# Moving the transposes of q, k and the masked scores from TensorE to the DMA crossbar in an attention and tanh-shrink kernel

## The chip, the cores and the metric

The kernel runs on one core of a Trainium2 chip. The metric is the device time of one execution in microseconds. A time is the median of the executions named with it. Nearly all executions here are fast. Where one or two of them were slow, the text says so and compares the fast ones.

## The reference

Eight batches of eight heads, 576 positions, 64 columns a head. Scores more than `tau` below their row's maximum are masked out, the rest go through a softmax. The output is the input of two layers with `h - tanh(h)` between them.

```python
scores = scale * np.matmul(q, k.transpose(0, 1, 3, 2))          # scale = 1/8
thresh = np.max(scores, axis=-1, keepdims=True) - tau           # tau = 0.02
scores = np.where(scores >= thresh, scores, -1000000000.0)
scores = scores - np.max(scores, axis=-1, keepdims=True)
attn = np.exp(scores); attn = attn / (np.sum(attn, axis=-1, keepdims=True) + 1e-09)
x = np.matmul(attn, v)                                          # then heads side by side: 4608 x 512
h = x @ w_in                                                    # 512 x 2048
out = (h - np.tanh(h)) @ w_out                                  # 2048 x 512
```

## The kernel before

Heads are taken in 32 pairs, each of nine score tiles: four of 128 rows for each head ("A" and "B" in turn, a duo), and a middle one, "M", with the last 64 rows of both. A row of scores has 576 columns. For exactness q and k are split into a high and a low fp16 half, side by side in 128 columns, and the scores add the products with `kT` and with `kS`, which is `kT` with its halves exchanged.

TensorE turns q and k by transposes into PSUM, VectorE copies them to SBUF, and two small DMAs make `kS`:

```python
def turn(p, t):
    hl = hls.pop((p, t))
    ps = ps_big.tile([P, W], FP16, name=f"ps_{t}", tag="big")          # W = 1152
    for c in range(TPP):                                               # TPP = 9
        nc.tensor.matmul(out=ps[:, c * P : (c + 1) * P], lhsT=..., rhs=ident_f16, is_transpose=True, ...)
    m = qk_pool.tile([P, W], FP16, name=f"{t}T", tag=t)
    nc.vector.tensor_copy(out=m, in_=ps)
    ...                                                                # first pair: cut
    elif t == "k":
        nc.sync.dma_start(out=sw[0:D, :], in_=m[D:P, :])
        nc.sync.dma_start(out=sw[D:P, :], in_=m[0:D, :])
```

A row maximum gives the threshold; `kink` writes the masked scores `z` (kept columns are score minus threshold, the others hugely negative). `weights` transposes `z` on TensorE into the single PSUM buffer `psZ`, and ScalarE takes the exponential from there:

```python
def weights(i):
    ps = ps_z.tile([P, 5 * P], BF16, name="psZ", tag="z")
    ...
    for c in range(n):                                                 # n = 4 or 5
        nc.tensor.matmul(out=ps[:, c * P : (c + 1) * P], lhsT=z[...], rhs=ident_bf, is_transpose=True, ...)
    nc.scalar.activation(out=pt[:, off : off + n * P], in_=ps[:, 0 : n * P], func=ACT.Exp)
```

One slot of the main loop handles one tile: scores three tiles ahead, `kink` one ahead, `weights`, a share of the layers of the batch before (from pair 4 on), and the product with v. All loads and stores go through the SP queue, but for the very first load of q.

Of the kernel before, what the change touches and what calls it, by code (L numbers as in the profile page):

```python
# [9 lines left out]
F32 = mybir.dt.float32  # L10
# [8 lines left out]
def kernel(  # L19
# [33 lines left out]
    AHEAD = 3  # L53
# [7 lines left out]
    ident_f16 = const.tile([P, P], FP16, name="ident_f16")  # L61
    make_identity(nc, ident_f16)
# [3 lines left out]
    xT = const.tile([P, DM_C, B, S], BF16, name="xT")  # L66
# [5 lines left out]
    NV = 3  # L72
# [8 lines left out]

    pool = lambda name, bufs, **kw: ctx.enter_context(
# [5 lines left out]
    qk_pool = pool("qk", 2)  # L88
    sc_pool = pool("sc", AHEAD + 1)
    st_pool = pool("st", 8)  # L90
    z_pool = pool("z", 3)
# [5 lines left out]
    y_pool = pool("y", 2)  # L97
    ps_big = pool("ps_big", 2, space=PSUM)
    ps_z = pool("ps_z", 1, space=PSUM)
    ps_o = pool("ps_o", 1, space=PSUM)  # L100
    ps_h = pool("ps_h", 1, space=PSUM)
# [9 lines left out]
    def load(p):  # L111
        b, h0 = p // HPAIR, 2 * (p % HPAIR)
        hs = slice(h0, h0 + 2)
        for t, src in (("k", k), ("q", q)):
            eng = nc.scalar if p == 0 and t == "q" else nc.sync
            r = raw_pool.tile([P, 10, D], F32, name=f"{t}raw", tag=t)
            eng.dma_start(
                out=r.rearrange("p (h c) d -> p h (c d)", h=2)[:, :, 0 : 4 * D],
                in_=src[b, hs, 0:512, :].rearrange("h (p c) d -> p h (c d)", c=4),
            )  # L120
            eng.dma_start(out=r[:, 4, :], in_=src[b, hs, 512:S, :])
            raws[p, t] = r
        r = raw_pool.tile([P, 10, D], F32, name="vraw", tag="v")
        nc.sync.dma_start(
            out=r[:, 0:8, :].rearrange("p (h c) d -> p h (c d)", h=2),
            in_=v[b, hs, 0:512, :].rearrange("h (p c) d -> p h (c d)", c=4),
        )
        rem = v[b, hs, 512:S, :].rearrange("h s d -> s h d")
        nc.sync.dma_start(out=r[0:64, 8:10, :], in_=rem)
        nc.sync.dma_start(out=r[64:P, 8:10, :], in_=rem)  # L130
        raws[p, "v"] = r
# [3 lines left out]
    def split(p, t, fast=False):  # L135
        r = raws.pop((p, t))[:, 0:9, :]
        hl = hl_pool.tile([P, TPP, 2, D], FP16, name=f"{t}hl", tag=t)
# [6 lines left out]
        else:  # L144
            x = hl_pool.tile([P, TPP, D], F32, name="xs", tag="xs")
# [7 lines left out]
        hls[p, t] = hl  # L153

    def split_v(p):
        r, vb = raws.pop((p, "v")), vbs[p % NV]
        nc.gpsimd.tensor_copy(
            out=vb[:, :, 0:4, 0:D],
            in_=r[:, 0:8, :].rearrange("p (h c) d -> p h c d", h=2),
        )  # L160
        nc.gpsimd.tensor_copy(out=vb[0:64, :, 4, 0:D], in_=r[0:64, 8:10, :])
        nc.gpsimd.tensor_copy(out=vb[64:P, :, 5, 0:D], in_=r[64:P, 8:10, :])
# [5 lines left out]
    def turn(p, t):  # L168
        hl = hls.pop((p, t))
        ps = ps_big.tile([P, W], FP16, name=f"ps_{t}", tag="big")  # L170
        for c in range(TPP):
            nc.tensor.matmul(  # L172
                out=ps[:, c * P : (c + 1) * P],
                lhsT=hl[:, c, :, :].rearrange("p a d -> p (a d)"),
                rhs=ident_f16, is_transpose=True, start=True, stop=True,
            )
        m = qk_pool.tile([P, W], FP16, name=f"{t}T", tag=t)
        nc.vector.tensor_copy(out=m, in_=ps)  # L178
        mats[p, t] = m
        if t == "k" and p == 0:  # L180
            ps = ps_big.tile([P, W], FP16, name="ps_ks", tag="big")
            for c in range(TPP):
                for a in range(2):
                    nc.tensor.matmul(
                        out=ps[64 * a : 64 * a + 64, c * P : (c + 1) * P],
                        lhsT=hl[:, c, 1 - a, :],
                        rhs=ident_f16, is_transpose=True, start=True, stop=True,
                    )
            sw = qk_pool.tile([P, W], FP16, name="kS", tag="ks")
            nc.vector.tensor_copy(out=sw, in_=ps)  # L190
            mats[p, "ks"] = sw
        elif t == "k":
            sw = qk_pool.tile([P, W], FP16, name="kS", tag="ks")
            nc.sync.dma_start(out=sw[0:D, :], in_=m[D:P, :])
            nc.sync.dma_start(out=sw[D:P, :], in_=m[0:D, :])
            mats[p, "ks"] = sw
# [4 lines left out]
    scs, zs, pts, ops = {}, {}, {}, {}  # L201
# [5 lines left out]
    def scores(i):  # L207
# [29 lines left out]
        )  # L237
        nb = st_pool.tile([P, 1], F32, name="nb", tag="nb")
# [5 lines left out]
    def kink(i):  # L244
        sc, nb = scs.pop(i)
        kd = kind(i % TPP)
        if kd == "B":
            z = zs[i - 1][:, S:W]
        else:
            zt = z_pool.tile([P, W], BF16, name="z")  # L250
            zs[i] = zt
            z = zt[:, 0:S]
        nc.scalar.activation(  # L253
            out=z, in_=sc, func=ACT.Prelu, bias=nb, scale=1.0, alpha=STEEP
        )

    def weights(i):

        kd = kind(i % TPP)
        ps = ps_z.tile([P, 5 * P], BF16, name="psZ", tag="z")  # L260
        if kd == "B":
            z, pt, off, n = zs.pop(i - 1), pts[i - 1], 512, 5
        else:
            z = zs[i] if kd == "A" else zs.pop(i)
            pt = p_pool.tile([P, TPP * P], FP16, name="pT")
            pts[i] = pt
            off, n = 0, 4
        for c in range(n):
            nc.tensor.matmul(  # L269
                out=ps[:, c * P : (c + 1) * P],  # L270
                lhsT=z[:, off + c * P : off + (c + 1) * P],
                rhs=ident_bf, is_transpose=True, start=True, stop=True,
            )
        if kd == "M":
            nc.tensor.matmul(
                out=ps[0:64, 512:640], lhsT=z[:, 512:576],
                rhs=ident_bf, is_transpose=True, start=True, stop=True,
            )
        nc.scalar.activation(  # L279
            out=pt[:, off : off + n * P], in_=ps[:, 0 : n * P], func=ACT.Exp  # L280
        )
        if kd == "M":
            nc.scalar.activation(
                out=pt[0:64, 512:640], in_=ps[0:64, 512:640], func=ACT.Exp
            )

    def attend(i):
# [19 lines left out]
        pt, hh = pts.pop(i - 1), int(j > 4)  # L307
# [24 lines left out]

    def emit_x(p):
        o = osb.pop(p)
        ps = ps_z.tile([P, S], BF16, name="psX", tag="z")
# [13 lines left out]
        nc.vector.tensor_copy(out=xT[:, p % HPAIR, b, :], in_=ps)  # L349


    gs = {}

    def hidden(m, n, ps):
        if n == 0:
            gs[m] = g_pool.tile([P, DF_C, MB], BF16, name="g")
        for c in range(DM_C):
            nc.tensor.matmul(  # L358
                out=ps, lhsT=w_in_sb[:, c, n * P : (n + 1) * P],
                rhs=xT[:, c, m, 0:MB] if m < B else xT[:, c, :, MB:S],  # L360
                start=(c == 0), stop=(c == DM_C - 1),
            )
        th = t_pool.tile([P, MB], F32, name="th")
        nc.scalar.activation(out=th, in_=ps, func=ACT.Tanh)  # L364
        nc.vector.scalar_tensor_tensor(  # L365
            out=gs[m][:, n, :], in0=th, scalar=-1.0, in1=ps,
            op0=ALU.mult, op1=ALU.add,
        )

    def project(m, ms, part, ps, last):  # L370
# [5 lines left out]
        if part == 3:  # L376
# [5 lines left out]
            if m < B:  # L382
                rows = out[m * S : m * S + MB, :].rearrange("(p c) n -> c p n", c=4)
                nc.sync.dma_start(out=rows[ms], in_=yo)
            else:
                rows = out.rearrange("(b s) n -> b s n", b=B)
                nc.sync.dma_start(out=rows[2 * ms : 2 * ms + 2, MB:S, :], in_=yo)

    def layers(m, tail):
# [3 lines left out]
        def h_step(n):  # L393
            if tail and n % 3:
                ps = ps_big.tile([P, MB], F32, name="psHt", tag="big")
            else:
                ps = ps_h.tile([P, MB], F32, name="psH", tag="h")
            hidden(m, n, ps)

        def y_step(ms, part):  # L400
            if part == 0:
                tag = ("y", "o", "z")[(4 * (m - 1) + ms) % 3] if tail else "y"
                pl = {"y": ps_y, "o": ps_o, "z": ps_z}[tag]
# [38 lines left out]

    load(0)
    load(1)
    for t in ("k", "q"):
        split(0, t, fast=True)
        turn(0, t)
# [6 lines left out]
    for s in range(-AHEAD, NTILE + 4):  # L454
        p, j = divmod(max(s, 0), TPP)
        if 0 <= s < NTILE and j == 3 and p % HPAIR == 0 and p >= HPAIR:
            assert not todo
            todo = layers(stage, False)
            share = len(todo) / (HPAIR * TPP - 3)
            done, stage = 0.0, stage + 1  # L460
        if s + AHEAD < NTILE:
            scores(s + AHEAD)
        if 0 <= s + 1 < NTILE:
            kink(s + 1)
# [9 lines left out]
        if s - 1 == NTILE + 1:  # L474
            emit_x(NPAIR - 1)
        if 0 <= s - 1 < NTILE:
            attend(s - 1)
            pp, jj = divmod(s - 1, TPP)
# [4 lines left out]
            if jj == 1 and pp > 0:  # L483
                emit_x(pp - 1)
        if 0 <= s < NTILE:
            if j == 0 and p + 2 < NPAIR:
                load(p + 2)
            if p + 1 < NPAIR:
                if j == 0:
                    split(p + 1, "k")  # L490
                if j == 1:
                    split(p + 1, "q")
                if j == 2:
                    split_v(p + 1)
                    turn(p + 1, "k")
                if j == 4:
                    turn(p + 1, "q")
            if s in w_when:
# [6 lines left out]
    while stage <= NMB:  # L505
        for step in layers(stage, True):
            step()
        stage += 1
# [37 lines left out]
```

## Time and profile before

| | before |
|---|---|
| time | 646.99 us, median of 4 (646.28 to 647.18) |
| span of the profile | 644.8 us |
| mean granted TensorE clock | 0.99 |
| first copy of a pair's output to the transposed x | 34.7 us |
| pace, pairs 8 to 31 | about 17.8 us a pair |
| end of attention, then layers only | 560 us, then 85 us |

The copies of a pair's output to the transposed x (`xT`, one for each pair) serve as milestones: the time between two of them is the pace. The lines of this profile stand in the prediction. A line of a group ends with busy us, mean ns of one instruction, and the idle time of the engine before them with what ended it.

### The profile page before, as it was taken

The numbers are of one execution on the slowest core, as the hardware profiler recorded it, in microseconds if no ns is written. First come the engines' busy times: TensorE is split into PE (matmuls) and PEld (weight loads), VectorE is DVE, ScalarE is ACT, GpSimd is POOL, SyncE is SP. The second block draws the span as 40 slices with busy tenths as digits, with TensorE's granted clock in tenths as the row PEclk, the third lists the DMA queues.
The fourth block names the chain that finished last, engine by engine and source line by source line (L and its number), as shares of the span: only waits on it lengthen the run. The fifth ranks groups of instructions, "written<-read, shape, count | busy, mean of one in ns | idle before, by whom it ended". The sixth has DMA issues, their size and how long they took to land.

```text
span 644.8 us, 15693 instructions
## 1 busy us (share of the span) xinstructions
PE 594.6 (92%) x6048; PEld 362.0 (56%) x6130; DVE 459.5 (71%) x1274; ACT 461.6 (72%) x761; POOL 215.2 (33%) x309
## 2 busy tenths in 40 slices
PE   2988998989999999999999999999999999999990
PEld 2666655556566566656655656656665666544440
DVE  2888888887877777877778777877877777544410
ACT  1888888887778777787778787777778778533410
POOL 6267557733303730343313630362133400000000
PEclk9999999999999999999999999999999999999996
DMA  5565656432223331353133231353134201000111
GB/s 152 155 177 163 175 168 174 119 81 73 64 65 91 104 93 37 93 148 92 40 87 84 77 90 38 93 149 95 36 93 121 66 17 37 18 33 34 49 36 47
DMA packets 57139, 57.35 MB, mean 89 GB/s; under 512 B 20840, under 2 KB 45416, under 8 KB 57064
## 3 DMA queue, kind: packets, MB, share of 16 engines
q1 hardware_dynamic: 56662, 56.05, 30.8%
q8 instruction: 48, 0.79, 0.5%
q10 hardware_dynamic: 402, 0.29, 0.1%
q14 instruction: 27, 0.22, 0.1%
HBM read 37.75 MB, written 9.44 MB: 73 GB/s over the span
## 4 chain that ended last, share of the span: by engine, by line
PE 79%; ACT 9%; DVE 4%; issue 3%; DMA 2%; SPq 1%; ACTq 0%
PE psY L372 18%; PE psH L358 16%; PE psS L228 16%; PE psZ L269 10%; PE psO L313 5%; ACT pT L279 5%; ACT z L253 3%; PE ps_k L172 3%; PE psHt L358 3%; PE ps_q L172 2%; PE psS L218 2%; DVE sc L234 2%; PE psX L337 2%; DMA out_dram<-yo 2%; PE psO L301 1%
## 5 line engine op out<-in xcount | busy, mean ns | idle before, releaser
L279 ACT ACTIVATE pT<-psZ 128x512 f16<-128x512 bf16 (+1 forms) x288 | 184.6, 641 | 83.8 <-PE psZ L269 80.9
L253 ACT ACTIVATE z<-sc,nb 128x576 bf16<-128x576 f32 x288 | 221.3, 768 | 8.9 <-DVE nb L239 8.9
L234 DVE TENSOR_SCALAR_CACHE_REDUCE sc<-psS 128x576 f32<-128x576 f32 x288 | 216.2, 751 | 8.8 <-PE psS L228 7.8
L365 DVE SCALAR_TENSOR_TENSOR g<-th,psH 128x512 bf16<-128x512 f32 x124 | 85.3, 688 | 88.9 <-ACT th L364 88.9
L372 PE MATMUL psY<-w_out_sb,g 128*128 128x512 bf16 x540 | 138.2, 379 | 1.3
L269 PE MATMUL psZ<-ident_bf,z 128*128 128x128 bf16 x1280 | 118.8, 219 | 9.9 <-ACT pT L279 9.1
L358 PE MATMUL psH<-xT,w_in_sb 128*128 128x512 bf16 x451 | 118.1, 379 | 3.4 <-issue 1.3
L269 PEld LDWEIGHTS <-z 128*128 128x128 bf16 x1280 | 79.2, 98 | 52.2 <-issue 16.7
L228 PE MATMUL psS<-kT,qT 128*128 128x512 f16 (+1 forms) x512 | 105.8, 288 | 2.8 <-DVE qT L178 0.9
L228 PEld LDWEIGHTS <-qT 128*128 128x128 f16 x1024 | 74.2, 98 | 58.8 <-issue 5.2
L228 PE MATMUL psS<-kS,qT 128*128 128x512 f16 (+1 forms) x512 | 105.6, 288 | 0.0
L364 ACT ACTIVATE th<-psH 128x512 f32<-128x512 f32 x124 | 74.0, 597 | 35.9 <-PE psH L358 34.3
L146 POOL TENSOR_SCALAR xs<-kraw 128x576 f32<-128x576 f32 x31 | 20.8, 670 | 225.0 <-DMA kraw<-in_k_dram 159.1
L372 PEld LDWEIGHTS <-g 128*128 128x128 bf16 x576 | 51.8, 98 | 46.1
L358 PEld LDWEIGHTS <-w_in_sb 128*128 128x128 bf16 x576 | 51.0, 98 | 43.0 <-issue 0.8
L313 PEld LDWEIGHTS <-pT 128*128 128x128 f16 x1280 | 55.8, 98 | 22.4
L313 PE MATMUL psO<-vb,pT 128*128 128x65 bf16 x1280 | 61.2, 193 | 0.9
L239 DVE TENSOR_SCALAR nb<-mx 128x1 f32<-128x1 f32 x288 | 44.3, 154 | 10.0
L150 POOL TENSOR_TENSOR khl<-xs,khl 128x576 f16<-128x576 f32 x31 | 39.7, 1279 | 2.6
L150 POOL TENSOR_TENSOR qhl<-xs,qhl 128x576 f16<-128x576 f32 x31 | 39.6, 1279 | 2.6
L328 DVE TENSOR_TENSOR osb<-psO,rc 128x320 bf16<-128x320 f32 x64 | 29.3, 458 | 2.2
L178 DVE COPY qT<-ps_q 128x1152 f16<-128x1152 f16 x32 | 24.1, 754 | 9.2 <-PE ps_q L172 9.2
(53 smaller groups left out, 462.3 us busy)
## 6 DMA issues: line engine op xcount, KB each, us to landing
out_dram<-yo SPq DMA_DIRECT2D x36, 256.0 KB
kS<-kT SPq DMA_DIRECT2D x62, 144.0 KB
kraw<-in_k_dram SPq DMA_DIRECT2D x32, 256.0 KB
vraw<-in_v_dram SPq DMA_DIRECT2D x32, 256.0 KB
qraw<-in_q_dram SPq DMA_DIRECT2D x31, 256.0 KB
wt<-in_moe_w_in_dram SPq DMA_DIRECT2D x8, 512.0 KB
wt<-in_moe_w_out_dram SPq DMA_DIRECT2D x8, 512.0 KB
vraw<-in_v_dram SPq DMA_DIRECT2D x64, 32.0 KB
```

The costliest lines, as they stand in the source:

```text
L150: nc.gpsimd.tensor_tensor(out=hl[:, :, 1, :], in0=x, in1=hl[:, :, 0, :], op=ALU.subtract)
L228: nc.tensor.matmul(out=ps[:, dst], lhsT=lhs, rhs=kk[:, src], start=(n == 0), stop=(n == 1),)
L234: nc.vector.tensor_scalar(out=sc, in0=ps[:, lo : lo + S], scalar1=SC, scalar2=None, op0=ALU.mult, op1=ALU.max, accum_out=mx,)
L239: nc.vector.tensor_scalar(out=nb, in0=mx, scalar1=-1.0, scalar2=tau, op0=ALU.mult, op1=ALU.add)
L253: nc.scalar.activation(out=z, in_=sc, func=ACT.Prelu, bias=nb, scale=1.0, alpha=STEEP)
L269: nc.tensor.matmul(out=ps[:, c * P : (c + 1) * P], lhsT=z[:, off + c * P : off + (c + 1) * P], rhs=ident_bf, is_transpose=True, start=True ...
L279: nc.scalar.activation(out=pt[:, off : off + n * P], in_=ps[:, 0 : n * P], func=ACT.Exp)
L313: nc.tensor.matmul(out=po[:, (j - 1 - 5 * hh) + ab, :], lhsT=pt[:, blk * P : (blk + 1) * P], rhs=vb[:, hh, c, :], start=(n == 0), stop=(n ...
L358: nc.tensor.matmul(out=ps, lhsT=w_in_sb[:, c, n * P : (n + 1) * P], rhs=xT[:, c, m, 0:MB] if m < B else xT[:, c, :, MB:S], start=(c == 0), ...
L364: nc.scalar.activation(out=th, in_=ps, func=ACT.Tanh)
L365: nc.vector.scalar_tensor_tensor(out=gs[m][:, n, :], in0=th, scalar=-1.0, in1=ps, op0=ALU.mult, op1=ALU.add,)
L372: nc.tensor.matmul(out=ps, lhsT=gs[m][:, n, ms * P : (ms + 1) * P], rhs=w_out_sb[:, n, :], start=(n == 0), stop=(n == DF_C - 1),)
```

## The change

The intent is to take all these transposes off TensorE and to leave it the products and the transposes of the output (psX). Each duo of masked scores, and k and q of each pair, are transposed by one DMA from SBUF to SBUF on the SP queue. VectorE writes k with its halves exchanged beside k, so that one transpose gives `kT` and `kS`. The exponential then reads SBUF, 1152 columns at a time. Because a DMA takes longer, everything runs further ahead (scores seven tiles, masks five). Loads cover four heads, for every second pair, and go to the GpSimd queue, so that they do not stand between the transposes.

```diff
-    AHEAD = 3
+    AHEAD = 7
+    MASK = 5
+    LAG = 2
...
     def load(p):
-        hs = slice(h0, h0 + 2)
+        hs = slice(h0, h0 + 4)
-            eng = nc.scalar if p == 0 and t == "q" else nc.sync
+            eng = nc.gpsimd if p else nc.sync if t == "k" else nc.scalar
...
+    def swap(p):
+        hl = hls[p, "k"]
+        for a in range(2):
+            nc.vector.tensor_copy(out=hl[:, 1, :, a, :], in_=hl[:, 0, :, 1 - a, :])
...
     def turn(p, t):
-        (nine transposes on TensorE, a copy on VectorE, two DMAs for kS)
+        m = qk_pool.tile([P, n, W], FP16, name=f"{t}T", tag=t)          # n = 2 for k, 1 for q
+        nc.sync.dma_start_transpose(
+            out=m.rearrange("p a (c n) -> p (a c) n", n=P),
+            in_=hl.rearrange("p a c h d -> p (a c h d)"),
+        )
...
     def kink(i):
+        if kd != "A":
+            n = 5 if kd == "M" else TPP
+            t = zt_pool.tile([P, TPP, P], BF16, name="zT")
+            nc.sync.dma_start_transpose(out=t[:, 0:n, :], in_=zt)
...
     def weights(i):
-        (four or five transposes to psZ, then the exponential of 512 or 640 columns)
+        if kd != "A":
+            nc.scalar.activation(out=pt[:, 0 : n * P], in_=zts.pop(i)[:, 0:n, :], func=ACT.Exp)
...
+    LD = 12                                                             # loads 12 slots before a pair's first scores
+    PREP = ((10, split k), (8, split q), (7, swap), (6, turn k), (5, turn q), (9, split_v))
```

The freed bank of PSUM goes to a second buffer for the hidden layer, and stores are issued a slot later. The tail's order changes slightly.

## The prediction

> **What bounds the kernel now.** I read the page's busy shares and the slices first, then the chain that ended last, then the groups, and last two close views of the steady state, because the change swaps one resource (TensorE) for another (the DMA engines) and the question is what is left over when TensorE is relieved.
>
> The busy shares and the slices of the page:
>
> ```profile
> PE 594.6 (92%) x6048; PEld 362.0 (56%) x6130; DVE 459.5 (71%) x1274; ACT 461.6 (72%) x761; POOL 215.2 (33%) x309
> ...
> PE   2988998989999999999999999999999999999990
> ...
> PEclk9999999999999999999999999999999999999996
> DMA  5565656432223331353133231353134201000111
> ...
> q1 hardware_dynamic: 56662, 56.05, 30.8%
> ```
>
> TensorE is busy from the second slice to the last at full clock; VectorE and ScalarE stand at seven tenths, and the DMA engines at five or six tenths in the first quarter (weights are loaded there) and about three tenths later. The queue moved 56.05 MB in 30.8% of 644.8 us, 198.6 us of all 16 engines: 282 GB/s while busy.
>
> The chain that ended last, shares by engine and by line:
>
> ```profile
> PE 79%; ACT 9%; DVE 4%; issue 3%; DMA 2%; SPq 1%; ACTq 0%
> PE psY L372 18%; PE psH L358 16%; PE psS L228 16%; PE psZ L269 10%; PE psO L313 5%; ACT pT L279 5%; ACT z L253 3%; PE ps_k L172 3%; PE psHt L358 3%; PE ps_q L172 2%; PE psS L218 2%; DVE sc L234 2%; PE psX L337 2%; DMA out_dram<-yo 2%; PE psO L301 1%
> ```
>
> The end is set by TensorE, and 15% of the chain (psZ, ps_k, ps_q) is transposes. These are the groups that the change removes or alters:
>
> ```profile
> L279 ACT ACTIVATE pT<-psZ 128x512 f16<-128x512 bf16 x160 | 94.8, 592 | 26.1 <-PE psZ L269 23.8 <-PE psZ L275 2.3
> L279 ACT ACTIVATE pT<-psZ 128x640 f16<-128x640 bf16 x128 | 89.8, 702 | 57.7 <-PE psZ L269 57.2
> L283 ACT ACTIVATE pT<-psZ 64x128 f16<-64x128 bf16 x32 | 8.3, 258 | 0.0
> ```
>
> ```profile
> L269 PE MATMUL psZ<-ident_bf,z 128*128 128x128 bf16 x1280 | 118.8, 219 | 9.9 <-ACT pT L279 9.1
> ...
> L178 DVE COPY qT<-ps_q 128x1152 f16<-128x1152 f16 x32 | 24.1, 754 | 9.2 <-PE ps_q L172 9.2
> L178 DVE COPY kT<-ps_k 128x1152 f16<-128x1152 f16 x32 | 24.1, 753 | 3.5 <-PE ps_k L172 1.2
> ...
> L172 PE MATMUL ps_k<-ident_f,khl 128*128 128x128 f16 x288 | 22.1, 223 | 9.0 <-DVE khl L140 9.0
> L172 PE MATMUL ps_q<-ident_f,qhl 128*128 128x128 f16 x288 | 21.7, 222 | 1.8 <-DVE qhl L140 1.8
> ```
>
> The copies of the output of pairs of heads to the transposed x in the timeline give the pace: 13.0 us from pair to pair for pairs 0 to 3 (no layers beside them), 16.1 us for pairs 4 to 7, and 17.8 us for pairs 8 to 31. The attention ends at about 560 us; a tail of 85 us has only layers. Four steady pairs in the windows view:
>
> ```profile
> core 0: us, PE busy (x) PEld busy (x) DVE busy (x) ACT busy (x) POOL busy (x), PEclk, DMA share, GB/s
> 138.12:209.21 71.09, 69.51 (x739) 43.08 (x749) 55.57 (x156) 55.97 (x93) 18.93 (x27) 1.00 0.29 77
> ```
>
> Per pair that is PE 17.4, DVE 13.9, ACT 14.0 of 17.8 us. So relief of TensorE is worth at most about 4 us a pair before ACT and DVE stop it.
>
> **What the Trainium skill says.** (1) "Trainium Kernel Development and Optimization", Performance Expectations: matmul busy time is a bad measure, since matmuls overlap. The trace agrees: a transpose is listed at 219 ns, but starts follow every 0.057 us (below). (2) "VectorE: DVE Perf Modes", The three transpose paths: 390 ns for a 128x128 bf16 block on TensorE, 1309 ns by the DMA crossbar, which ends in SBUF. The first isn't what this trace shows in a stream (219 ns, overlapped); no run here shows the second yet. (3) "DMA: Bandwidth & Descriptors", Latency and other measured facts: a DMA transpose moves 261 GB/s with a non-contiguous middle dimension, 350 to 400 if contiguous. The plain copies here reach 282. I take 300 as an estimate between. (4) The same page, Issuing engines are not separate DMA queues: all issuers share 16 engines, so the GpSimd queue for loads saves only SP's issue time. The trace fits: one queue carries nearly all traffic.
>
> **The change part by part, for one steady pair (9 tiles).**
>
> *TensorE.* The timeline, start to start, since durations overlap:
>
> ```profile
> 308.97 0.44 PE L269 MATMUL psZ<-ident_bf,z 128*128 128x128 bf16 x5
> ...
> 309.25 1.03 PE L372 MATMUL psY<-w_out_sb,g 128*128 128x512 bf16 x4
> ...
> 316.22 0.68 PE L172 MATMUL ps_k<-ident_f,khl 128*128 128x128 f16 x9
> ...
> 316.73 0.41 PE L228 MATMUL psS<-kT,qT 128*128 128x512 f16 x2
> ```
>
> Five transposes hold TensorE 0.28 us, nine 0.51; four hold 0.23 and the middle tile's five 0.49 elsewhere in the same stretch. A pair has 4 x 0.23 + 4 x 0.28 + 0.49 + 2 x 0.51 = 3.55 us of transposes. 17.4 - 3.55 = 13.8 us stays. (The groups' busy times would promise 5.4 us; that is the overlap.)
>
> *ScalarE.* The exponentials of a duo, 592 + 702 ns, become one of 1152 columns. 128 more columns cost 110 ns, so 0.86 ns a column and 592 + 640 x 0.86 = 1142 ns: 0.15 us saved, five times a pair (the middle tile saves 592 + 258 - 702). Reading SBUF instead of PSUM may give 0.03 each back. 14.0 - 0.75 + 0.15 = 13.4 us.
>
> *VectorE.* kT and qT copies go (1.51 us). Two swap copies of 576 fp16 columns come: 0.3 us each, an estimate between a 4-fold and a 1-fold rate. The copy of x in two pieces adds 0.1. 13.9 - 1.51 + 0.6 + 0.1 = 13.1 us.
>
> *DMA.* Transposed bytes a pair: four duos of 128x1152x2 (1180 KB), the middle tile padded to 640 columns (164), k with its swapped form (590), q (295): 2.23 MB in seven transposes. At 300 GB/s 7.4 us. Loads of q, k, v 0.92 MB and a store of 0.26 MB at 282 GB/s: 4.2 us. Together 11.6 us of the engines, four times today's share, but under the 13.8. The two kT to kS copies fall away.
>
> *GpSimd.* 6.3 us of casts a pair (25.2 in a neighbouring window of four) plus about six load issues; hidden unless an issue costs well over 1 us.
>
> So PE, ACT and DVE come to lie within 0.7 us of each other, with DMA close below. Today's pace is 0.4 us over PE's busy time; with four near-equal resources I take 0.7 over the largest: 14.5 us. 24 pairs x (17.8 - 14.5) = 79 us saved.
>
> *Pairs 0 to 7.* 8.4 MB of weights come in over some 7.5 pairs, 1.1 MB or 4 us a pair. DMA: 7.4 + 3.3 + 4.0 = 14.7 us for pairs 0 to 3 against a pace of 13.0 today (+7), and about 14.4 for pairs 4 to 7 against 16.1 (-7). Sum 0: here the DMA engines are the bound.
>
> *Start and end.* The first scores start at 15.0 us. The first loads are twice as large (0.59 MB more, 2 us), and seven tiles of scores instead of three precede the first weights (4 tiles x 1 us), with two DMA latencies: +8. At the end the last duo goes through a DMA and one more slot of lag: +5. The tail is TensorE alone and keeps its length.
>
> Sum: 647 + 8 + 0 - 79 + 5 = 581; I say 580.
>
> **Rivals.** (a) *The crossbar becomes the bound.* For it: 2.23 MB a pair is much, and SP takes the transposes in order, so a late one delays all behind it. Against: loads were taken off that queue, and z is made five slots ahead, over 7 us. At 200 GB/s the DMA needs 11.1 + 4.2 = 15.3 us a pair; pace 15.8, pairs 0 to 7 at 18.4: 647 + 31 - 48 + 13 = 643, no change. At 130 GB/s it is 21 us a pair and near 800 us. The 1309 ns for one block can't hold block after block (68 blocks a pair would be 89 us), so I read it as mostly fixed cost. (b) *The engines run at their floors.* If transposes reach 350 GB/s and waits between PE and ACT (80.9 us for pT today, off ACT's critical path) go, pace 13.9 and DMA 13.6 in the early pairs: -94, -8, +10, about 555. (c) *GpSimd is the bound*: load issues of several us delay the splits of k and q, which delay the transposes; pace 16: about 615.
>
> **Range and chances.** 540 covers (b) with a little to spare, 625 covers (c) and a transpose rate of some 220 GB/s. Outcome (a) in full is what can make it slower; depths chosen with such care (seven ahead, mask five ahead) speak for a rate that is good enough. Faster 0.87, same 0.07, slower 0.06.
>
> **What would show it.** Right: the PE share falls to about 80%, no PE transposes but psX; exponentials at about 1.15 us; swaps at 0.2 to 0.4 us; steady pace 14 to 15 us with PE, ACT and DVE each over 85% busy; DMA share over 0.75; first pairs no faster than before. Wrong: waits of pT on the transposed z or of psS on kT that fill each pair, an SP queue never idle, a pace over 15.5 us, or a GpSimd at over 90%.

## The result, and the profile after

| | before | after |
|---|---|---|
| time | 646.99 us | 712.54 us, median of 4 (706.65 to 725.73, the last slow) |
| span of the profile | 644.8 us | 704.9 us |
| mean granted TensorE clock | 0.99 | 0.87 |

The ratio is 1.098, with a 95% interval of 1.091 to 1.106. Ratios are the mean time of one kernel's fast runs over that of the other's from the same rounds, so they are not quite the ratios of the medians quoted. The change makes the kernel about 10% slower.

The milestones divide the 60.1 us by which the span grew:

| stretch | before | after | predicted | measured |
|---|---|---|---|---|
| start to the first xT | 34.7 | 52.9 | +8 | +18.2 |
| first to eighth xT | 103.4 | 126.6 | 0 | +23.2 |
| eighth to last xT (24 pairs) | 422.1 | 441.3 | -79, +5 at its end | +19.2 |
| last xT to the end | 84.6 | 84.1 | 0 | -0.5 |

The page of the changed kernel: busy shares (PE is TensorE, PEld its weight loads, DVE VectorE, ACT ScalarE, POOL GpSimd, SPq the issuing on SP), the clock and the DMA engines by slice, then the two main DMA queues (packets, MB, share of 16 engines' span).

```profile
PE 515.2 (73%) x4155; PEld 265.2 (38%) x4224; DVE 420.5 (60%) x1310; ACT 439.9 (62%) x601; POOL 307.3 (44%) x446
...
PEclk9767767888889796998979798979889799999996
DMA  5999999999988999798999999999989999601011
...
q1 hardware_dynamic: 294968, 89.75, 70.1%
q0 software_dynamic: 9568, 28.19, 16.9%
```

TensorE, VectorE and ScalarE are all far from full, and the DMA engines are busy from the second slice to the end of the attention. The chain that ended last, by engine and by line, now runs through DMAs and their issue on SP:

```profile
PE 39%; DMA 28%; SPq 11%; POOL 9%; issue 4%; ACT 4%; DVE 2%; POOLq 0%; ACTq 0%; DVEq 0%
```

The pace is not even. From pair to pair it goes 25.2, 12.9, 25.7, 14.9 us, and so in turn from about the eighth pair until the loads end; each long pair is one in which GpSimd has issued the loads of four heads. The windows view of these four pairs:

```profile
core 0: us, PE busy (x) PEld busy (x) DVE busy (x) ACT busy (x) POOL busy (x), PEclk, DMA share, GB/s
299.62:324.84 25.22, 16.94 (x130) 8.43 (x131) 12.45 (x42) 14.82 (x22) 13.30 (x20) 0.80 1.07 184
324.84:337.75 12.91, 12.04 (x119) 6.58 (x120) 11.88 (x40) 10.91 (x15) 5.03 (x8) 1.00 0.85 160
337.75:363.41 25.66, 15.68 (x128) 7.97 (x128) 12.40 (x42) 14.62 (x21) 13.01 (x20) 0.80 1.07 184
363.41:378.30 14.89, 14.68 (x133) 7.82 (x135) 13.22 (x42) 12.49 (x18) 5.82 (x9) 1.00 0.89 154
```

In the short pairs the kernel runs as predicted, TensorE over 90% busy at full clock. In the long ones all engines but the DMA have holes. (Packet times overlap, so a DMA share can pass 1; it is 1.08 for transposes alone in the measuring program below. So it is not pure work.) What happens in a long pair is seen in the timeline of GpSimd, of SP and of TensorE; columns are start and duration in us, and the idle time before with its releaser in brackets.

```profile
299.97 0.82 POOL L127 DMA_DIRECT2D kraw<-in_k_dram  x1
...
305.35 0.62 POOL L143 DMA_DIRECT2D vraw<-in_v_dram  x1
```

```profile
304.27 9.39 SPq L191 DMA_TRANSPOSE kT<-khl  x1
313.75 1.74 SPq L191 DMA_TRANSPOSE qT<-qhl  x1
...
327.70 2.15 SPq L191 DMA_TRANSPOSE kT<-khl  x1
```

```profile
318.55 1.14 PE L229 MATMUL psS<-kT,qT 128*128 128x512 f16 x4 [7.95 <-DMA qT<-qhl]
```

GpSimd issues 1.84 MB of loads between 300 and 306 us. The transpose of k, issued at 304.3, holds SP for 9.4 us; in the next pair, without loads, it holds it for 2.2. The transpose of q stands behind it, the scores behind both, and TensorE idles 7.95 us. It then comes back at half clock: the four matmuls take 1.14 us, and 0.65 at other times. "TensorE: Matmul & The Clock Gate" of the Trainium skill (Why this matters for your kernels) warns of idle gaps over some 3 us for this; the trace agrees, with a granted clock of 0.50 from 315 to 320 us. The waits view of the whole run (us in total, times, longest) has the same three at the top of what DMAs held up:

```profile
POOL khl L166 <- DMA kT<-khl: 156.5, 19, 12.8
PE psS L229 <- DMA qT<-qhl: 151.0, 22, 16.7
ACT pT L278 <- DMA zT<-z: 127.4, 27, 9.2
```

### The profile page after: what moved, and what is told of

Same layout as the page of the kernel before. It is cut to its first block, busy times and chain, and to the rows that moved or that the text cites. A ratio compares the mean times of both kernels' runs of the same rounds, so it can differ in the third digit from the quotient of the medians.

```text
span 704.9 us, 11975 instructions
## 1 busy us (share of the span) xinstructions
PE 515.2 (73%) x4155; PEld 265.2 (38%) x4224; DVE 420.5 (60%) x1310; ACT 439.9 (62%) x601; POOL 307.3 (44%) x446
## 3 DMA queue, kind: packets, MB, share of 16 engines
q0 software_dynamic: 9568, 28.19, 16.9%
## 4 chain that ended last, share of the span: by engine, by line
PE 39%; DMA 28%; SPq 11%; POOL 9%; issue 4%; ACT 4%; DVE 2%; POOLq 0%; ACTq 0%; DVEq 0%
PE psY L385 12%; DMA qT<-qhl 12%; PE psS L229 11%; SPq L191 10%; DMA kraw<-in_k_dram 10%; PE psH L359 8%; PE psO L309 3%; POOL xs L163 2%; POOL qhl L167 2%; PE psHt L359 2%; ACT z L261 2%; ACT pT L278 2%; DMA out_dram<-yo 1%; DMA zT<-zm 1%; DMA vraw<-in_v_dram 1%
## 5 line engine op out<-in xcount | busy, mean ns | idle before, releaser
L229 PE MATMUL psS<-kT,qT 128*128 128x512 f16 (+1 forms) x1024 | 189.1, 318 | 160.6 <-DMA qT<-qhl 151.0
L278 ACT ACTIVATE pT<-zT 128x1152 f16<-128x1152 bf16 (+1 forms) x160 | 170.9, 1068 | 127.6 <-DMA zT<-z 127.4
L261 ACT ACTIVATE z<-sc,nb 128x576 bf16<-128x576 f32 x256 | 193.4, 765 | 47.0 <-DVE nb L244 46.2
L229 PEld LDWEIGHTS <-qT 128*128 128x128 f16 x1024 | 78.6, 105 | 239.1 <-DMA qT<-qhl 157.2
L385 PE MATMUL psY<-w_out_sb,g 128*128 128x512 bf16 x532 | 145.1, 393 | 4.8 <-issue 3.9
L359 PE MATMUL psH<-xT,w_in_sb 128*128 128x512 bf16 x456 | 126.4, 395 | 1.5 <-issue 0.2
L166 POOL CAST khl<-xs 128x576 f16<-128x576 f32 x31 | 20.5, 662 | 167.0 <-DMA kT<-khl 156.5
L359 PEld LDWEIGHTS <-w_in_sb 128*128 128x128 bf16 x576 | 50.1, 101 | 61.2 <-issue 11.6
L394 DVE COPY yo<-psY 128x512 f32<-128x512 f32 x30 | 20.7, 690 | 18.6 <-PE psY L385 8.8
L178 POOL CAST vb<-vraw 128x512 bf16<-128x512 f32 x32 | 20.1, 629 | 22.0 <-PE psO L309 9.6
L163 POOL TENSOR_SCALAR xs<-kraw 128x576 f32<-128x576 f32 x31 | 21.1, 679 | 19.2 <-DMA kraw<-in_k_dram 17.8
L261 ACT ACTIVATE zm<-sc,nb 128x576 bf16<-128x576 f32 x32 | 24.7, 771 | 6.3 <-DVE nb L244 5.7
```

Of the source, the lines that this page charges most:

```text
L229: nc.tensor.matmul(out=ps[:, dst], lhsT=lhs, rhs=kk[:, src], start=(n == 0), stop=(n == 1),)
L261: nc.scalar.activation(out=z, in_=sc, func=ACT.Prelu, bias=nb, scale=1.0, alpha=STEEP)
L278: nc.scalar.activation(out=pt[:, 0 : n * P], in_=zts.pop(i)[:, 0:n, :], func=ACT.Exp)
L359: nc.tensor.matmul(out=ps, lhsT=w_in_sb[:, c, n * P : (n + 1) * P], rhs=xs[m][:, c, :] if m < B else xR[:, c, :, :], start=(c == 0), stop= ...
L385: nc.tensor.matmul(out=ps, lhsT=gs[m][:, n, ms * P : (ms + 1) * P], rhs=w_out_sb[:, n, :], start=(n == 0), stop=(n == DF_C - 1),)
```

## The experiments

Twelve kernels were run. The two measuring programs and the kernel without loads give wrong results; all others are correct. The pace is that of the profiled run, from the eighth to the 28th xT.

| run | what | time us | ratio to before | pace us |
|---|---|---|---|---|
| (changed kernel) | | 712.5 | 1.098 | 19.5 |
| e_noload | loads after the first left out | 575.2 | 0.888 | 14.2 |
| e_load2 | GpSimd loads, two heads, 16 slots ahead | 749.9 (fast: 740.4, 744.9) | 1.158 | 20.3 |
| e_ld16 | GpSimd loads 16 slots ahead | 737.6 (fast: 734.7 to 739.3) | 1.137 | (slow profile) |
| e_load_sp | loads on the SP queue | 657.8 | 1.017 | 16.9 |
| e_sp16 | the same, 16 slots ahead | 652.0 | 1.008 | 17.2 |
| e_kq_pe | k, q back on TensorE | 680.4 | 1.052 | 18.8 |
| e_z_pe | masked scores back on TensorE | 693.1 | 1.067 | 19.0 |
| e_zpe_sp16 | e_z_pe, loads on SP, 16 ahead | 649.1 | 1.003 | 17.4 |
| e_kqpe_sp16 | e_kq_pe, loads on SP, 16 ahead | 607.5 | 0.940 | 15.7 |
| e_kqpe_l2sp | the same, loads of two heads | 597.7 | 0.924 | 15.1 |

### What the crossbar moves by itself

The first theory was volume (V): the crossbar is slower than the 300 GB/s that I took. Its rival was the burst (B): loads of four heads at once hold up transposes that are fast enough.

```diff
+    for t in outs: nc.sync.dma_start_transpose(out=t, in_=src[:, 0:1152])      # 12 in a row, and other stretches
```

> A measuring program with a wrong result on purpose: gated stretches with 1 duo transpose of 128x1152 fp16 alone, then 12 of them in a row (3.54 MB), 6 of the k form 128x2304 (3.54 MB), 12 plain copies of 128x1152 from SBUF to SBUF (3.54 MB), 6 loads of four heads (512 KiB each, 3.15 MB) from the GpSimd queue, the same from the SP queue, then 12 transposes beside the GpSimd loads, and 12 beside loads from the ScalarE queue. Theory V (volume: the crossbar itself is slow): 12 transposes alone take 17 us or more (under 210 GB/s), and beside loads the time is about the sum of the two alone. Theory B (burst: a load burst holds up the transposes, which alone are fast): alone 13.5 us or less (over 260 GB/s), and beside the GpSimd loads clearly more than the sum.

The times are VectorE's waits for the last landing of a stretch. For one duo alone VectorE waited 3.7 us (the DMA itself landed 3.3 us after its issue). For twelve in a row it waited 19.8 us, so each further one takes 1.46 us, (19.8 - 3.7) / 11, which is 0.295 MB at 202 GB/s. The six transposes of k's form took 19.3 us for the same bytes. Twelve plain copies of the same tile took 11.3 us. So V's number is met: a crossbar transpose is slower than a plain copy. What sets the 202 GB/s is open: the issue of a duo holds SP for 1.3 to 1.5 us, alone (1.36 us) as well as in a row, so it may be SP's issuing as well as the crossbar. The stretch with GpSimd loads was not cleanly divided from the loads before it, so the mix was measured again, later.

### Without the loads

```diff
     def load(p):
+        if p:
+            (the tiles of the first four heads are used again)
+            return
```

> All loads of q, k and v after the first four heads are left out and the first heads are used again (wrong result on purpose); the 16 weight loads stay. Both theories expect a large gain, since transposes then have the DMA engines nearly alone: a steady pace of 14 to 14.5 us a pair, the pace of the changed kernel's quick pairs now, and 560 to 600 us. If the transposes alone fill the DMA engines (V in its strong form, 165 GB/s as their packet times read, 13.5 us a pair plus stores), the DMA share stays near 0.9 and waits on qT stay. If the time stays over 660 us, neither is right, and the order on the SP queue alone is the bound.

The time is 575.2 us (two runs) and the pace 14.2 us. Both theories expected that; what it tells is how much of the loss hangs on the loads. The windows view over four pairs of this kernel (columns as above):

```profile
299.00:356.00 57.00, 55.50 (x516) 29.85 (x525) 51.09 (x163) 52.98 (x74) 25.31 (x36) 1.00 0.95 176
```

Per pair this is PE 13.9, DVE 12.8, ACT 13.2 us. All transposes still go through the crossbar here, so these alone do not make the kernel slow. Loads of 0.92 MB a pair cost 5.3 us a pair, 19.5 - 14.2.

### Smaller loads, and earlier loads, on the same queue

```diff
-        hs = slice(h0, h0 + 4)            # for every second pair, 12 slots ahead
+        hs = slice(h0, h0 + 2)            # for each pair, 16 slots ahead, GpSimd queue as before
```

> Loads still on the GpSimd queue and of the same bytes, but of two heads for each pair and four or more slots earlier, in place of four heads for every second pair. Theory B: the alternation of 13 and 25 us pairs goes, since no burst is due just before its use; pace about 14.5 to 16 us, total 600 to 645 us. Theory V: the alternation goes, but the pace stays near the sum of the DMA work, 17 to 19 us, total 670 to 710 us.

749.9 us, but two of the four executions were slow. The fast two, 740.4 and 744.9 us, are still slower than the change itself (705.9 to 714.5 in its fast runs) and outside both theories' ranges. They are 14.7% over the kernel before; the table's 1.158 fits all four. The alternation goes, as both said, but not into an even pace: most pairs now take 16 to 25 us. If only the size of a burst or its lead mattered, this would have helped. So B falls in the form I gave it.

### Fewer bytes on the crossbar

```diff
     def turn(p, t):                       # as in the kernel before
+        nine transposes on TensorE, a copy on VectorE, two DMAs for kS
```

> k and q are transposed on TensorE again as in the kernel before (with the two small kT to kS copies), only the masked scores go through the crossbar; loads stay. Transposed bytes fall from 2.23 to 1.34 MB a pair, TensorE gets 1.0 us a pair back, VectorE 1.5 minus the swaps. Theory V: pace 15.5 to 16.5 us, 620 to 650 us. Theory B: the burst still holds z's transposes but no longer the scores' start; 610 to 660 us. Both expect clearly less than the changed kernel's 712; at 700 or over the transposes of k and q, which stand in the chain, would not be the cause.

680.4 us, again above both ranges: 40% fewer bytes on the crossbar gave 32 us.

### The mix, measured properly

Neither theory explained that plenty of loaded stretches of the changed kernel ran at 177 to 200 GB/s. Two readings were left: the two kinds add up (A), or mixing them loses time (M).

```diff
+    24 transposes alone; 12 loads alone; both together, with the loads on the GpSimd, ScalarE or SP queue
```

> A measuring program with a wrong result on purpose; stretches divided by gates: 24 duo transposes alone (7.08 MB), 12 loads of 512 KiB alone from the GpSimd queue (6.29 MB), the same alone from the ScalarE queue, then the 24 transposes beside the 12 loads from the GpSimd, the ScalarE and the SP queue, then 24 plain copies of the same tile alone and beside the GpSimd loads. The first measuring run had the transposes alone at 201 GB/s and loads up to 350. Theory A (additive: both kinds only share the engines' time): 35 us alone, about 20 for the loads, 52 to 57 us for each of the mixes. Theory M (mixing loses time: a load's long pieces and a transpose's short ones hold each other up): 62 us or more for the mix from the GpSimd queue, as the 177 to 200 GB/s in the loaded stretches of the changed kernel suggest (13.4 MB at 190 GB/s is 70 us); if it is the GpSimd queue's own doing, the mix from the SP queue stays near 55.

24 transposes alone took 36.9 us, 12 loads from GpSimd alone 22.0. Together they took 55.0 us with GpSimd loads, 58.6 with ScalarE's and 58.0 with SP's (each from the first issue until VectorE, which waits for the last landing, goes on). The last two are a little over A's range, and none is near M's 62: in this program A holds, and no time is lost against the sum, 58.9. But who waits is quite different. The transposes' lines of the tile view, for the stretch alone, that beside GpSimd loads, and that beside loads on SP; the times are min/median/max, the first in ns of the issue on SP, the second in us to landing:

```profile
L42 SPq DMA_TRANSPOSE tp<-src x24: 1342/1404/1504, 4.4 to 37.7; - x24
DMA to landing us min/median/max: 3.3/3.5/3.5
...
L42 SPq DMA_TRANSPOSE tp<-src x24: 1243/1402/12792, 88.9 to 139.8; - x24
DMA to landing us min/median/max: 3.3/3.5/19.7
...
L42 SPq DMA_TRANSPOSE tp<-src x24: 1242/1814/2965, 206.2 to 258.3; - x24
DMA to landing us min/median/max: 4.1/4.8/5.1
```

And the windows view in the stretch with GpSimd loads (the last number is GB/s):

```profile
100.00:104.00 4.00, 0.00 (x0) 0.74 (x1) 1.00 1.05 353
104.00:108.00 4.00, 0.00 (x0) 0.00 (x0) 1.00 1.04 351
...
116.00:120.00 4.00, 0.00 (x0) 0.00 (x0) 1.00 1.06 202
120.00:124.00 4.00, 0.00 (x0) 0.00 (x0) 1.00 1.07 200
```

While the GpSimd loads last, the engines run at 351 to 353 GB/s, the rate that loads reach alone (339 to 349 in their own stretch); then at 200 to 202, near the rate of transposes alone (204). So the loads went first and the transposes waited: SP got three of them issued in the first 17.6 us. This I call starvation, theory S. With the loads in the SP queue the transposes land in at most 5.1 us, and with the loads from ScalarE's queue in at most 12.9. "DMA: Bandwidth & Descriptors" (Queues, rings and completion order) says that each engine takes its rows of queues in turn, a whole packet at a time; that lets the queue with the larger packets take more. The trace of this program agrees. Its transposes move in packets of 256 bytes and its GpSimd loads in packets of 4096, and while both are in flight the two queues move equally many packets. The DMA view of 98 to 110 us gives the first two lines (queue: packets, MB, share of 16 engines). The last two are the stretch where plain copies, in packets of 2304 bytes, stand beside the same loads (292 to 316 us):

```profile
q0 software_dynamic: 1082, 3.92, 94.4%
q1 hardware_dynamic: 1080, 0.27, 10.9%
...
q0 software_dynamic: 1501, 5.44, 65.2%
q1 hardware_dynamic: 1491, 3.06, 37.1%
```

One packet for one, the transposes get 6% of the bytes and the copies 36%.

The kernel is less simple than this program. The trace of the changed kernel has ten bursts of loads from 182 us on. From the first issue of a burst to its last landing, 14 to 20 us, the engines moved only 153 to 214 GB/s, transposes and stores 49 to 90 of them, with six to twelve packets of the SP queue to one of the loads. At 350 GB/s for the loads and 202 for the rest, the same bytes would take 9 to 12 us. So in the kernel the mix does lose time, as M said, and turns by packet do not account for it. The measuring program, in which the other engines stood nearly idle, does not show why.

### The loads in the same queue as the transposes

```diff
-            eng = nc.gpsimd if p else nc.sync if t == "k" else nc.scalar
+            eng = nc.scalar if p == 0 and t == "q" else nc.sync      # and v on nc.sync
```

> The changed kernel with all loads of four heads on the SP queue, in order with the transposes, in place of the GpSimd queue; nothing else. Theory M with the GpSimd queue at fault: the loads no longer run beside the transposes, so the mix loses nothing: pace 14.5 to 16.5 us, 600 to 650 us. Theory A: the same engine time in another order, so about as the changed kernel, 690 to 730 us, or worse because later transposes queue behind the loads.

657.8 us, 55 us less than the change, with the same bytes, the same transposes and the same lead. Only the queue differs, and what comes with it: the loads then move in packets of 1024 bytes in place of 4096, and SP issues them in place of GpSimd. It is still 1 to 2% slower than the kernel before. It missed the range given under "the GpSimd queue at fault", by 8 us, and is far below that of the other. The tile view of the transposes of k, first the changed kernel, then this one:

```profile
L191 SPq DMA_TRANSPOSE kT<-khl x32: 2112/4006/11782, 11.4 to 587.9; - x32
```

```profile
L191 SPq DMA_TRANSPOSE kT<-khl x32: 1925/2490/3889, 11.0 to 537.8; - x32
```

The longest hold falls from 11.8 to 3.9 us, the median from 4.0 to 2.5. The pace still alternates, about 13 to 15 and 19 to 21 us.

### Masked scores on TensorE, k and q by the crossbar

```diff
     def weights(i):                       # as in the kernel before, with psZ; loads still on GpSimd
```

> The masked scores are transposed on TensorE again as in the kernel before (one bank of PSUM moves from the hidden layer to them), only k and q go through the crossbar; loads stay as in the changed kernel. Crossbar bytes fall from 2.23 to 0.885 MB a pair, 4.4 us at 201 GB/s, so with loads and a store the DMA needs under 10 us a pair. Theory A and M both: the DMA is no longer the bound, TensorE's is 17.4 - 1.0 = 16.4 us a pair; pace 16.6 to 17.2 us, 605 to 635 us, faster than the kernel before by 2 to 6%. At 660 or over, the chain from a load through split and transpose to the scores, not the sum of the DMA work, sets the pace.

693.1 us (one of the four executions was slow, 694.9). The DMA share is about five tenths, so the sum of the DMA work is out of the question here, and the case foreseen for 660 and over holds: the chain sets the pace. In a slow pair of its chain the transpose of q takes 11.9 us.

### Lead against starvation, and the two halves with the loads on SP

First, lead alone:

```diff
-    LD = 12
+    LD = 16                               # loads on the GpSimd queue, as in the change
```

> The changed kernel with its loads still on the GpSimd queue but asked for 16 slots ahead in place of 12. Theory S (starvation: bytes and mixing cost nothing extra, but transposes in flight wait until the loads of another queue have drained, as in the measuring run, where the landing rose from 3.5 to 19.7 us beside GpSimd loads and stayed under 5.2 us with the loads on SP): the stall of 10 us every second pair stays, wherever the loads stand: 690 to 725 us. Theory L (lead: the loads come too late for the splits, since the chain goes load, split, transpose, scores): 650 us or less.

737.6 us, with one of four executions slow; the fast three took 734.7 to 739.3 us. More lead makes it worse, beyond even S's range. Theory L falls.

The same lead with the loads on SP:

```diff
-    LD = 12
+    LD = 16                               # on top of e_load_sp
```

> Loads of four heads on the SP queue (as in e_load_sp, 657.8 us) and 16 slots ahead in place of 12. Theory S and L together: in e_load_sp the chain ran through the load of v, which landed after its slot; with four slots more that wait goes: pace 15 to 16 us, 605 to 640 us. If lead does not matter, it stays at 655 to 660.

652.0 us against 657.8: a miss of the range, and near "lead does not matter". (Its profile is that of the slowest of its four runs, 657.4 us, so its pace of 17.2 is not slower than e_load_sp's 16.9 for sure.) The chain still runs through the load of v (9% of the span) and the transpose of q (7%).

```diff
+    e_z_pe, loads on nc.sync, LD = 16
```

> As e_z_pe (masked scores on TensorE, k and q by the crossbar; 693.1 us) but with the loads on the SP queue, 16 slots ahead. Theory S: e_z_pe was slow with half the DMA time unused because kT and qT took 12 us beside GpSimd loads; on the SP queue they take under 6: pace 16.8 to 17.4 us, 610 to 640 us. If it stays over 670, starvation by the GpSimd queue was not e_z_pe's trouble.

649.1 us, 44 less than with GpSimd loads 12 slots ahead (queue and lead changed at once), and the same as the kernel before within 2%. The median landing of qT falls from 6.5 to 3.2 us and its longest from 15.5 to 4.9. The pace of 17.4 us is the upper end of what was expected, the time above it. TensorE is the bound (89% busy, 68% of the chain), and ScalarE waits for the single psZ as in the kernel before (66 us).

```diff
+    e_kq_pe, loads on nc.sync, LD = 16
```

> As e_kq_pe (k and q on TensorE, masked scores by the crossbar; 680.4 us) but with the loads on the SP queue, 16 slots ahead. Theory S: pace 15 to 16 us, 590 to 625 us, possibly the best of all, since TensorE needs 14.8 us and the DMA 10.7 us a pair. Over 650: the order on the SP queue (masked scores behind loads and copies of kT) is a bound of its own.

607.5 us, 6% faster than the kernel before. Queue and lead changed at once against e_kq_pe; since lead alone did harm in e_ld16 and nearly nothing in e_sp16, I put the 73 us down to the queue, but they were not parted here.

### The best version

```diff
-        hs = slice(h0, h0 + 4)            # loads of four heads for every second pair
+        hs = slice(h0, h0 + 2)            # for each pair, on nc.sync, 16 slots ahead; k and q on TensorE
```

> As e_kqpe_sp16 (607.5 us: k and q on TensorE, masked scores by the crossbar, loads on the SP queue), but with loads of two heads for each pair in place of four for every second pair, still 16 slots ahead. If the bursts that remain (nine issues of 0.6 us in a row on SP, with the masked scores' transposes behind them) still cost something, the pace falls from 15.7 to about 15.2 us and the time to 590 to 603 us; if the pace is TensorE's own by now, 603 to 612; more than 615 would say that more and smaller DMAs in one queue cost more than the bursts.

597.7 us, ratio 0.924: bursts still cost 10 us, and this version beats both kernels. Its page's busy shares and the first line of its chain:

```profile
PE 524.8 (88%) x4800; PEld 287.8 (48%) x4800; DVE 441.0 (74%) x1310; ACT 439.5 (74%) x601; POOL 216.2 (36%) x310
...
PE 72%; DMA 8%; DVE 5%; issue 4%; POOL 4%; ACT 3%; SPq 2%; ACTq 0%; POOLq 0%
```

TensorE sets the end again, with fewer transposes to do. The same two-head loads on the GpSimd queue had made the change worse (e_load2).

## Why the prediction was wrong

**The engines' part was right.** The floors of 13.8, 13.1 and 13.4 us for TensorE, VectorE and ScalarE are 13.9, 12.8 and 13.2 in the kernel without loads, and its pace is 14.2 where 14.5 was predicted with them. An exponential of 1152 columns takes 1.15 us, as worked out; a swap copy 0.41 us in place of 0.3. The short pairs of the changed kernel run at that pace too. The tail kept its length. What failed was the DMA part, in two steps.

**"At 300 GB/s 7.4 us" was mis-sized.** The transposes move at 202 GB/s, so a pair's 2.23 MB takes 11.0 us, not 7.4. With loads of 0.92 MB at 350 GB/s (2.6 us, better than the 282 that I took) and a store of 0.26 MB at 382 GB/s (0.7 us, from the stores that end a measuring run), a pair needs 14.3 us of the DMA engines, not 11.6. So even by this sum, an estimate from rates measured apart, the DMA engines are as full as TensorE, not below it, and no slack remains to work off a wait. Rival (a) had this rate in it and made 643 us of it; e_load_sp, with the same work in one queue, has 657.8.

**"The GpSimd queue for loads saves only SP's issue time" was wrong, and with it "with four near-equal resources I take 0.7 over the largest".** I summed bytes and took their order as free. The trace that I quoted for it could not test it, since one queue carried 56.05 of 57.35 MB there. Beside loads from the GpSimd queue a transpose waits: it lands after up to 19.7 us in place of 3.5 in the measuring program, and k's holds SP for up to 11.8 us in the kernel. Only the queue differs between the change and e_load_sp: 55 us, or 2.7 us of pace (19.5 to 16.9). That the queue costs this is shown. How much of it is the loads going first, and how much the time that the mix loses in the kernel (bursts at 153 to 214 GB/s; 223 to 250 in e_load_sp from 175 us on), is not parted. The other 2.7 us down to the pace of 14.2 without loads are the loads' own DMA time, their issues on SP, and the order in that queue; no run parts these. The direction of rival (a) was right, as was its "a late one delays all behind it"; of the 70 us by which its 643 falls short, 55 go with the queue of the loads. Rival (c), GpSimd as the bound by slow issues, was not it: the issues took 0.6 to 0.8 us, and GpSimd was 44% busy.

**Pairs 0 to 7 and the start.** There the engines carry the weights as well, and the sum of 0 turned out as +23 us, probably by the same two causes; no run shows it for these pairs alone. At the start +18 came in place of +8: the first scores start at 16.7 us, near what was expected, but the first xT is copied five slots later by the deeper pipeline, in the slowest part. The two were not parted by a run.

**The clock.** I had not allowed for it: stalls of 8 us and more drop the granted clock, to 0.80 on average in the long pairs. That makes a stall cost more than its length; how much of the 132 us between prediction and result it is was not measured apart.

**The chances.** The care in the depths was taken as a sign that the rate sufficed. It was no evidence: the depths suit the landing of 3.5 us that a transpose has alone, and not the 10 to 20 us beside loads.

**What stays open.** Why e_load_sp and e_sp16 stop at about 17 us where DMA work and engines each need about 14.3. One rival was not tested: in e_load_sp the issues on SP fill 15.0 of the 16.9 us of a pair (11.7 transposes, 2.7 loads), in one queue that also waits for ScalarE to finish z (97 us in the whole run), so the order on SP may be the bound. Smaller loads on SP helped the version with k and q on TensorE by 10 us, but were not tried with all transposes on the crossbar. And why loads and transposes together move at only 153 to 214 GB/s in the kernel.

## What to carry to other kernels

A transfer that stands in the chain is to be judged by its landing beside the traffic that it meets, not by its bytes over a rate: loads from another queue can keep it waiting, here for 10 us and more. When a stage is moved to the DMA engines, first measure its rate alone and its landing beside the loads, and look in the timeline for a pace that alternates with the loads. With all loads on the SP queue and 16 slots ahead, moving only the part with slack (here the masked scores, five slots ahead) and keeping the part that opens the chain (k and q) where it was brought 6.0%, where moving all lost 0.8%. With smaller loads the first brought 7.6%.

## What the Trainium skill lacked or had wrong

- "DMA: Bandwidth & Descriptors", Latency and other measured facts: 261 GB/s for a DMA transpose, 350 to 400 when contiguous. From SBUF to SBUF these runs show 204 GB/s for contiguous rows of 1152 fp16 elements and 208 for 2304, while plain copies of the 1152-column tile reach 386. "Advanced Engine Details and Errata", X-Bar Transpose (TRN2), that such DMAs are as fast as regular ones, is not what these runs show.
- "DMA: Bandwidth & Descriptors", Issuing engines are not separate DMA queues: that they interleave is true of the sum in the measuring program (55 us for both, 36.9 and 22.0 alone). That the choice of the issuing engine saves only issue time is not what these runs show: the same loads on SP in place of GpSimd take 55 us off the kernel.
- The same page lacks what turns by packet mean for a transpose, whose packets are 256 bytes in these traces, beside 4096 for GpSimd loads and 1024 for loads from SP or ScalarE. In the measuring program transposes landed up to 19.7 us after issue beside GpSimd loads in place of 3.5, up to 12.9 beside ScalarE's, and 5.1 with all in one queue.
- The same page lacks that the time for which a transpose holds its issuing sequencer grows beside other traffic: 1.4 us for a duo alone, up to 12.8 us beside loads.
- "VectorE: DVE Perf Modes", The three transpose paths: 1309 ns for a 128x128 block by the crossbar. No run here times one block, but a single DMA of nine lands in 3.3 us, and in a row of such DMAs a block takes 0.16 us (1.46 / 9).
